# Setup in fixed order, grad_out requested by ScalarE, V0 in one load and head 31 stored in halves, in an attention backward kernel

## The chip, the cores and the metric

The kernel runs on one core of a Trainium2 chip. The metric is the device time of one execution in microseconds (us). Most executions agree within 0.3%, and every comparison is with runs of the kernel before on the same chip.

## The reference

Decode attention for 32 heads, one query row each, 8192 keys, width 128, all bfloat16, and its gradients:

```python
B, H, Sq, Skv, Dh = 1, 32, 1, 8192, 128
def _fwd_reference(q, k, v):
    scale = q.shape[-1] ** -0.5
    scores = jnp.einsum('bhqd,bhkd->bhqk', q, k) * scale
    attn = _softmax(scores, axis=-1)
    return jnp.einsum('bhqk,bhkd->bhqd', attn, v)
# returns out_0 = forward result, then the gradients for q, k, v:
_out, _vjp = jax.vjp(_f, q, k, v); _grads = _vjp(grad_out)
```

Per head K and V (2 MB each) are read, and dk and dv (2 MB each) are written. out and dq are one row per head.

## The kernel before

Each head: VectorE transposes K in four pieces, TensorE makes the scores, a softmax follows, TensorE transposes V (ScalarE copies it out of PSUM) and forms V·grad_out, and VectorE writes dv and dk as outer products. All transfers are asked for by SyncE, in one queue. The parts that the change and the argument touch:

```python
    def load_v(h):
        Vt[h] = vpool.tile([P, NT, D], BF16, tag="V", name="Vt")
        parts = NCH if h == 0 else 1                       # NCH = 4
        for c in range(parts):
            nc.sync.dma_start(slots(Vt[h], c, parts), rows_of(v, h, c, parts))

    rows = consts.tile([H, 2, D], BF16)
    nc.sync.dma_start(rows[:, 0, :], q.rearrange("b h s d -> (b h s) d"))
    nc.sync.dma_start(rows[:, 1, :], grad_out.rearrange("b h s d -> (b h s) d"))
    load_k(0); load_v(0); load_k(1); load_v(1)
    # ... setup: ident_f, ones_f, in_quad, lane; q columns (q_blk); grad_out columns
    #     (do_blk, do_f), all copies on VectorE; the scheduler chooses their order ...
    order = tc.manual_schedule()                           # from here on: order as written
    order.__enter__()

    def contract(Xt, rep, out_col, first=0, last=NT):      # o and dq: 64 one-column matmuls each
        for n in range(first, last):
            nc.tensor.matmul(out_col, lhsT=Xt[:, n, :], rhs=rep[:, n, 0:1],
                             start=(n == 0), stop=(n == NT - 1), skip_group_check=True)

    def outer(h, which, r):                                # quarter r of dk or dv
        # ... VectorE multiply into G ...
        parts = 4 if h == H - 1 else 2 if h == 0 else 1
        if r % (4 // parts) == 4 // parts - 1:
            c = r // (4 // parts)
            nc.sync.dma_start(rows_of(dst, h, c, parts), slots(G, c, parts))
```

## Time and profile before

| | before |
|---|---|
| time, median (range) | 649.27 us (648.69 to 650.84) |
| span in the profile | 647.3 us |
| HBM traffic, mean rate | 269.81 MB, 417 GB/s |
| TensorE, VectorE, ScalarE busy | 78%, 79%, 28% |
| last landing of a transfer | 646.28 us |

How to read it: in the lines, PE, DVE, ACT, POOL and SP are TensorE, VectorE, ScalarE, GpSimd and SyncE, and a q behind the name is the part of the engine that issues requests. K0 is K of head 0, V31 is V of head 31. The rate in forty slices tells where time is lost; the table of stretches with DMA share tells by how many DMA engines it is lost. The trace records sixteen landings for each large transfer, one for each DMA engine. I call the difference between the last and the first of them the lag. No view prints them one by one, so these are given as numbers. The lines themselves stand in the prediction.

### The profile page before, as it was taken

What the parts mean: (1) busy time and instruction counts of PE and PEld (TensorE: products, weight loads), DVE (VectorE), ACT (ScalarE), POOL (GpSimd) and SP (SyncE); (2) the same over time, 40 slices, a digit from 0 to 9 for tenths busy, and PEclk for the clock granted to TensorE, in tenths of its full rate; (3) what the DMA queues carried; (4) which work ended last, traced back from release to release, by engine and by line L of the source; (5) the groups of instructions that cost most, each with busy time, mean ns of one, the idle gap of its engine ahead of it and who ended that gap; (6) DMA issues with size and microseconds to landing.
All of it is one profiled execution on the core that took longest, in us unless ns stands there. A gap on an engine that the chain in (4) does not pass through costs nothing.

```text
span 647.3 us, 20978 instructions
## 1 busy us (share of the span) xinstructions
PE 505.1 (78%) x9705; PEld 472.7 (73%) x9705; DVE 513.1 (79%) x660; ACT 183.1 (28%) x325; POOL 0.7 (0%) x6
## 2 busy tenths in 40 slices
PE   2888888788968787888768787768887777977970
PEld 1888788688867777878668787668886776877870
DVE  5799889789977779777788777797777977778860
ACT  0333223223333222232222332222322223222240
POOL 0000000000000000000000000000000000000000
PEclk9866555556676555656565565575556666555565
DMA  8999999999999999999999999999999999999984
GB/s 329 413 425 428 424 427 427 426 426 425 428 427 429 426 429 426 431 424 430 425 430 426 431 424 430 430 425 422 426 425 429 427 430 425 427 431 428 409 367 201
DMA packets 20727, 269.81 MB, mean 417 GB/s; under 512 B 2464, under 2 KB 2464, under 8 KB 4512
## 3 DMA queue, kind: packets, MB, share of 16 engines
q1 hardware_dynamic: 20640, 268.48, 97.9%
q8 instruction: 76, 1.25, 0.7%
q14 instruction: 11, 0.09, 0.0%
HBM read 134.23 MB, written 134.23 MB: 415 GB/s over the span
## 4 chain that ended last, share of the span: by engine, by line
DMA 53%; PE 29%; DVE 11%; ACT 3%; issue 1%; SPq 0%; DVEq 0%; ACTq 0%
DMA Kt<-in_k_dram 48%; PE T_ps L179 10%; DVE XK_sb L141 8%; PE s_ps L153 6%; PE dp_ps L196 5%; DMA out_dram<-G_dv 5%; PE m_ps L196 2%; PE dp_ps L191 2%; ACT XT_sb L181 1%; PE s_ps L169 1%; PE m_ps L273 1%; PE m_ps L286 1%; DVE G_dv L206 1%; ACT e L285 1%; ACT qd L222 1%
## 5 line engine op out<-in xcount | busy, mean ns | idle before, releaser
L179 PE MATMUL T_ps<-ident_f,Vt 128*128 128x128 f32 x1024 | 220.4, 396 | 0.0
L206 DVE TENSOR_TENSOR G_dv<-p_rep,qd 128x2048 bf16<-128x2048 bf16 x128 | 148.2, 1221 | 68.5 <-DMA out_dram<-G_dv 66.0
L179 PEld LDWEIGHTS T_ps<-ident_f,Vt 128*128 128x128 f32 x1024 | 195.1, 216 | 0.0
L181 ACT COPY XT_sb<-T_ps 128x1024 f32<-128x1024 f32 x128 | 129.6, 1013 | 145.8 <-PE T_ps L179 145.8
L206 DVE TENSOR_TENSOR G_dk<-ds_rep,qd 128x2048 bf16<-128x2048 bf16 x128 | 155.8, 1219 | 1.1
L141 DVE STREAM_TRANSPOSE XK_sb<-Kt 128x1024 f32<-128x1024 f32 x128 | 148.1, 1214 | 5.6 <-DMA Kt<-in_k_dram 5.5
L153 PE MATMUL s_ps<-q_blk,XK_sb 128*128 128x4 bf16 x2048 | 59.6, 168 | 45.8 <-DVE pdt L227 43.0
L191 PEld LDWEIGHTS <-XT_sb 128*128 128x128 bf16 x2048 | 72.2, 105 | 28.6 <-ACT XT_sb L181 27.0
L191 PE MATMUL dp_ps<-do_blk,XT_sb 128*128 128x2 bf16 x2048 | 73.0, 165 | 24.3 <-ACT XT_sb L181 24.3
L153 PEld LDWEIGHTS <-XK_sb 128*128 128x128 bf16 x2048 | 57.1, 104 | 47.7 <-DVE pdt L227 44.9
L196 PE MATMUL dp_ps<-ds_rep,Kt 128*128 128x1 bf16 x2048 | 64.6, 165 | 3.8 <-issue 3.4
L196 PEld LDWEIGHTS <-Kt 128*128 128x128 bf16 x2048 | 59.8, 104 | 9.5 <-issue 9.4
L196 PEld LDWEIGHTS <-Vt 128*128 128x128 bf16 x2048 | 60.2, 101 | 1.6
L237 ACT COPY dq_all<-dp_ps 128x1 f32<-128x1 f32 x32 | 5.1, 159 | 193.4 <-PE dp_ps L196 193.4
L196 PE MATMUL m_ps<-p_rep,Vt 128*128 128x1 bf16 x2048 | 58.7, 165 | 0.0
L286 PEld LDWEIGHTS m_ps<-rs,ones_f 128*128 128x128 f32 x64 | 16.0, 309 | 48.6 <-ACT e L285 48.6
L286 PE MATMUL m_ps<-rs,ones_f 128*128 128x1 f32 x64 | 18.7, 361 | 39.2 <-ACT e L285 39.2
L273 PE MATMUL m_ps<-diag,ones_f 128*128 128x128 f32 x64 | 25.5, 499 | 2.0 <-issue 1.3
L282 DVE TENSOR_REDUCE nbias<-m_ps 128x1 f32<-128x128 f32 x32 | 9.3, 292 | 21.6 <-ACT qd L222 21.6
L295 ACT ACTIVATE p_rep<-e,rinv 128x256 bf16<-128x256 f32 x32 | 16.3, 508 | 30.3 <-DVE rinv L293 30.3
L222 ACT CAST qd<-m_ps 128x256 bf16<-128x256 f32 x32 | 11.9, 372 | 44.8 <-PE m_ps L218 44.8
L229 DVE SCALAR_TENSOR_TENSOR ds_rep<-dp_ps,pdt,p_s 128x256 bf16<-128x256 f32 x32 | 15.5, 484 | 10.3 <-PE dp_ps L191 8.0
(44 smaller groups left out, 155.1 us busy)
## 6 DMA issues: line engine op xcount, KB each, us to landing
Kt<-in_k_dram SPq DMA_DIRECT2D x31, 2048.0 KB, 30.8
Vt<-in_v_dram SPq DMA_DIRECT2D x31, 2048.0 KB, 28.2
out_dram<-G_dv SPq DMA_DIRECT2D x30, 2048.0 KB, 32.7
out_dram<-G_dk SPq DMA_DIRECT2D x30, 2048.0 KB, 33.0
Kt<-in_k_dram SPq DMA_DIRECT2D x4, 512.0 KB, 5.2
Vt<-in_v_dram SPq DMA_DIRECT2D x4, 512.0 KB, 8.1
out_dram<-G_dv SPq DMA_DIRECT2D x2, 1024.0 KB, 11.0
out_dram<-G_dk SPq DMA_DIRECT2D x2, 1024.0 KB, 12.4
```

Of the source, the lines that this page charges most:

```text
L141: nc.vector.transpose(XK[h][:, :, :, u, :], slots(Kt[h], u, NCH).rearrange("p g d -> p (g d)").bitcast(F32).rearrange("p (g w j) -> p g w ...
L153: nc.tensor.matmul(out[:, g, :], lhsT=cols[:, g, c // 2, c % 2], rhs=q_blk[:, h, c, :], start=(c == 0), stop=(c == 2 * NB - 1), skip_group ...
L179: nc.tensor.transpose(T_ps[:, i, :], words[:, m * P:(m + 1) * P], ident_f[:])
L181: nc.scalar.copy(X[:], T_ps[:])
L191: nc.tensor.matmul(st[h]["dp"][:, n:n + 2], lhsT=X[:, i, e2, :], rhs=do_blk[:, h, e2, :], start=(e2 == 0), stop=(e2 == 1), skip_group_chec ...
L196: nc.tensor.matmul(out_col, lhsT=Xt[:, n, :], rhs=rep[:, n, 0:1], start=(n == 0), stop=(n == NT - 1), skip_group_check=True)
L206: nc.vector.tensor_tensor(slots(G, r, 4).rearrange("p n (a b) -> p n a b", b=R), slots(rep, r, 4).unsqueeze(2).to_broadcast([P, Q, D // R, ...
L222: nc.scalar.copy(x["qd"][:].rearrange("p a d -> p (a d)"), x["m"][:, 256:512])
L229: nc.vector.scalar_tensor_tensor(out=x["ds"][:], in0=x["dp"][:, 0:NT].unsqueeze(2).to_broadcast([P, NT, R]), scalar=pdt[:], in1=x["p_s"][: ...
L273: nc.tensor.matmul(x["m"][:, 128:256], lhsT=ones_f[:], rhs=diag[:], start=True, stop=True, skip_group_check=True)
L286: nc.tensor.matmul(x["m"][:, 0:1], lhsT=ones_f[:], rhs=rs[:], start=True, stop=True, skip_group_check=True)
L295: nc.scalar.activation(x["p"][:], e[:].unsqueeze(2).to_broadcast([P, NT, R]), ACT.Copy, scale=rinv[:])
```

## The change

The intent: make the q columns while K0 is in flight and not in the middle of its transposes; take grad_out's request out of the way of K0's; move grad_out's columns to ScalarE; have fewer, larger requests at both ends.

```diff
     def load_v(h):
         Vt[h] = vpool.tile([P, NT, D], BF16, tag="V", name="Vt")
-        parts = NCH if h == 0 else 1
-        for c in range(parts):
-            nc.sync.dma_start(slots(Vt[h], c, parts), rows_of(v, h, c, parts))
+        nc.sync.dma_start(Vt[h][:], rows_of(v, h, 0, 1))
@@
-    nc.sync.dma_start(rows[:, 1, :], grad_out.rearrange("b h s d -> (b h s) d"))
+    nc.scalar.dma_start(rows[:, 1, :], grad_out.rearrange("b h s d -> (b h s) d"))
@@ the fixed order now begins ahead of the setup
+    order = tc.manual_schedule()
+    order.__enter__()
@@ q columns: four copies, four transposes into one PSUM tile, four products; (cut)
@@ grad_out columns: from VectorE to ScalarE, after head 0's scores
+    def do_columns():
+        for e2 in range(2):
+            nc.scalar.copy(twice[:, e2], ...)
+        ... three transposes ...
+        for e2 in range(2):
+            for t in range(2):
+                nc.scalar.copy(do_blk[t * W:(t + 1) * W, :, e2, t], ...)
+        nc.scalar.copy(do_f[:], tp[:, 2, 0:H])
@@ in outer()
-        parts = 4 if h == H - 1 else 2 if h == 0 else 1
+        parts = 1
+        if h == 0 or h == H - 1:
+            parts = 2
@@ in the loop over heads
+        if h == 0:
+            do_columns()
```

More of the change, by code (lines that the diff above doesn't have):

```diff
@@ L91 @@
     make_identity(nc, ident[:])
+    order = tc.manual_schedule()
+    order.__enter__()
+    ones_f = consts.tile([P, P], F32)
+    nc.vector.memset(ones_f[:], 1.0)
+    do_blk = consts.tile([P, H, 2, 2], BF16)
+    nc.vector.memset(do_blk[:], 0.0)
+    in_quad = consts.tile([P, NQ], F32)
+    nc.vector.reduce_sum(in_quad[:], ident[:].rearrange("p (a i) -> p a i", a=NQ), axis=AX.X)
+    q_blk = consts.tile([P, H, 2 * NB, NQ], BF16)
+    four = consts.tile([H, 2 * NB, NQ, QD], BF16)
+    for w in range(NB):
+        for e2 in range(2):
+            nc.vector.tensor_copy(
+                four[:, 2 * w + e2], rows[:, 0, :].rearrange("h (w j e) -> h w e j", w=NB, e=2)[:, w, e2:e2 + 1, :]
+                .to_broadcast([H, NQ, QD]))
@@ L92 @@
+    tp = psT.tile([P, CH, P], BF16, tag="T", name="tp_q")
+    for c in range(2 * NB):
+        nc.tensor.transpose(tp[:, c, 0:H], four[:, c].rearrange("h a j -> h (a j)"), ident[0:H, 0:H])
+    lane = consts.tile([P, QD], F32)
+    nc.vector.reduce_sum(lane[:], ident[:].rearrange("p (a i) -> p i a", a=NQ), axis=AX.X)
     ident_f = consts.tile([P, P], F32)
     nc.vector.tensor_copy(ident_f[:], ident[:])
-    ones_f = consts.tile([P, P], F32)
-    nc.vector.memset(ones_f[:], 1.0)
-    in_quad = consts.tile([P, NQ], F32)
@@ L97 @@
-    nc.vector.reduce_sum(in_quad[:], ident[:].rearrange("p (a i) -> p a i", a=NQ), axis=AX.X)
-    lane = consts.tile([P, QD], F32)
-    nc.vector.reduce_sum(lane[:], ident[:].rearrange("p (a i) -> p i a", a=NQ), axis=AX.X)
-    q_blk = consts.tile([P, H, 2 * NB, NQ], BF16)
-    for w in range(NB):
-        for e2 in range(2):
-            four = consts.tile([H, NQ, QD], BF16, tag=f"four{w}{e2}")
-            nc.vector.tensor_copy(
-                four[:], rows[:, 0, :].rearrange("h (w j e) -> h w e j", w=NB, e=2)[:, w, e2:e2 + 1, :]
-                .to_broadcast([H, NQ, QD]))
-            tp = psT.tile([P, CH, P], BF16, tag="T")
-            nc.tensor.transpose(tp[:, 0, 0:H], four[:].rearrange("h a j -> h (a j)"), ident[0:H, 0:H])
-            nc.vector.tensor_tensor(
-                q_blk[:, :, 2 * w + e2, :], tp[:, 0, 0:H].unsqueeze(2).to_broadcast([P, H, NQ]),
-                in_quad[:].unsqueeze(1).to_broadcast([P, H, NQ]), op=ALU.mult)
@@ L115 @@
-    do_blk = consts.tile([P, H, 2, 2], BF16)
-    nc.vector.memset(do_blk[:], 0.0)
-    for e2 in range(2):
-        twice = consts.tile([H, 2, W], BF16, tag=f"twice{e2}")
-        nc.vector.tensor_copy(
-            twice[:], rows[:, 1, :].rearrange("h (j e) -> h e j", e=2)[:, e2:e2 + 1, :].to_broadcast([H, 2, W]))
-        tp = psT.tile([P, CH, P], BF16, tag="T")
-        nc.tensor.transpose(tp[:, 0, 0:H], twice[:].rearrange("h t j -> h (t j)"), ident[0:H, 0:H])
-        for t in range(2):
-            nc.vector.tensor_copy(do_blk[t * W:(t + 1) * W, :, e2, t], tp[t * W:(t + 1) * W, 0, 0:H])
@@ L125 @@
-    do_f = consts.tile([P, H], F32)
-    tp = psT.tile([P, CH, P], BF16, tag="T")
-    nc.tensor.transpose(tp[:, 0, 0:H], rows[:, 1, :], ident[0:H, 0:H])
-    nc.vector.tensor_copy(do_f[:], tp[:, 0, 0:H])
+    for c in range(2 * NB):
+        nc.vector.tensor_tensor(
+            q_blk[:, :, c, :], tp[:, c, 0:H].unsqueeze(2).to_broadcast([P, H, NQ]),
+            in_quad[:].unsqueeze(1).to_broadcast([P, H, NQ]), op=ALU.mult)
+    twice = consts.tile([H, 2, 2, W], BF16)
+    do_f = consts.tile([P, H], F32)
@@ new lines, in do_columns @@
+    def do_columns():
+        for e2 in range(2):
+            nc.scalar.copy(
+                twice[:, e2], rows[:, 1, :].rearrange("h (j e) -> h e j", e=2)[:, e2:e2 + 1, :].to_broadcast([H, 2, W]))
+        tp = psT.tile([P, CH, P], BF16, tag="T", name="tp_do")
+        for e2 in range(2):
+            nc.tensor.transpose(tp[:, e2, 0:H], twice[:, e2].rearrange("h t j -> h (t j)"), ident[0:H, 0:H])
+        nc.tensor.transpose(tp[:, 2, 0:H], rows[:, 1, :], ident[0:H, 0:H])
+        for e2 in range(2):
+            for t in range(2):
+                nc.scalar.copy(do_blk[t * W:(t + 1) * W, :, e2, t], tp[t * W:(t + 1) * W, e2, 0:H])
+        nc.scalar.copy(do_f[:], tp[:, 2, 0:H])
@@ L130 @@
     o_all = consts.tile([P, H], F32)
     dq_all = consts.tile([P, H], F32)
-    order = tc.manual_schedule()
-    order.__enter__()
     def k_blocks(h, u):
```

## The prediction

> **What bounds the kernel now.** I read the page of the profile first. It moves 269.81 MB at a mean of 417 GB/s, while no compute engine is busy for more than 79% of the span.
>
> ```profile
> span 647.3 us, 20978 instructions
> PE 505.1 (78%) x9705; PEld 472.7 (73%) x9705; DVE 513.1 (79%) x660; ACT 183.1 (28%) x325; POOL 0.7 (0%) x6
> DMA  8999999999999999999999999999999999999984
> GB/s 329 413 425 428 424 427 427 426 426 425 428 427 429 426 429 426 431 424 430 425 430 426 431 424 430 430 425 422 426 425 429 427 430 425 427 431 428 409 367 201
> DMA 53%; PE 29%; DVE 11%; ACT 3%; issue 1%; SPq 0%; DVEq 0%; ACTq 0%
> ```
>
> The reader is to see a flat row of GB/s, about 427, between a poor first slice (329) and three poor last ones (409, 367, 201). At 427 GB/s the traffic needs 269.81 / 0.427 = 632 us of the 647.3, so all that the change can touch is some 15 us at the two ends. The DMA share of the chain of waits says the same of the middle.
>
> Next the timeline of the start, which is where most of the diff works:
>
> ```profile
> 1.19 0.41 SPq L84 DMA_DIRECT2D rows<-in_grad_out_dram  x1
> 1.65 1.85 SPq L74 DMA_DIRECT2D Kt<-in_k_dram  x4
> ...
> 5.53 2.52 DVE L141 STREAM_TRANSPOSE XK_sb<-Kt 128x1024 f32<-128x1024 f32 x2 [2.16 <-DMA Kt<-in_k_dram]
> ...
> 8.54 1.04 DVE L111 TENSOR_TENSOR q_blk<-tp,in_quad 128x128 bf16<-128x128 bf16 x4
> ...
> 10.76 2.36 DVE L141 STREAM_TRANSPOSE XK_sb<-Kt 128x1024 f32<-128x1024 f32 x2
> ```
>
> VectorE transposes half of K0, then makes the q and grad_out columns from 7.97 to 10.84, then the other half of K0: the setup sits in the middle of head 0. And grad_out's request delays K0's first request from 1.19 to 1.65 us.
>
> Then the timeline of the end, and the table of stretches over it:
>
> ```profile
> 620.47 4.63 DVE L206 TENSOR_TENSOR G_dv<-p_rep,qd 128x2048 bf16<-128x2048 bf16 x4 [2.98 <-DMA out_dram<-G_dv]
> ...
> 629.03 8.77 SPq L214 DMA_DIRECT2D out_dram<-G_dk  x4
> ...
> 638.69 0.33 SPq L246 DMA_DIRECT2D out_dram<-fin_sb  x1
> ```
>
> ```profile
> 638.00:640.00 2.00, 0.00 (x0) 0.00 (x0) 0.00 (x0) 0.00 (x0) 0.00 (x0) 0.50 0.95 381
> 640.00:642.00 2.00, 0.00 (x0) 0.00 (x0) 0.00 (x0) 0.00 (x0) 0.00 (x0) 0.50 0.42 172
> 642.00:644.00 2.00, 0.00 (x0) 0.00 (x0) 0.00 (x0) 0.00 (x0) 0.00 (x0) 0.50 0.13 52
> 644.00:646.00 2.00, 0.00 (x0) 0.00 (x0) 0.00 (x0) 0.00 (x0) 0.00 (x0) 0.50 0.05 21
> ```
>
> These four rows (last two columns: DMA share, GB/s) decide my prediction. Compute ended at about 632.4, the last large request went out at 637.5, and yet data moves until 645.7 with a share that sinks to 0.05. One engine of sixteen is 0.06, and one sixteenth of 427 GB/s is 27. So at the end a single DMA engine is still working off a backlog and the other fifteen are done. I checked it in the landing records of the trace, of which each transfer has sixteen. The first and the last of the sixteen are 0.6 us apart for K0, 2.1 for K2, 8.2 at 200 us, 17.0 for V31. And the last one never pauses: K31, the dk of head 29, V31, the dv of 30, the dk of 30 in two transfers are finished at 605.3, 610.5, 615.4, 620.4, 625.8, 631.3, 636.1 in the order of the queue, always about 5 us for 2 MB; then 512 KB quarters follow each other every 1.23 to 1.26 us up to 646.1. In the middle it is the same, 4.87 us for a load and 5.0 to 5.1 for a store. The dips at 612 to 620 and 628 to 640 us are those of the engines that ran ahead and had nothing left; the late one was never without work from 5 us on.
>
> So what bounds the kernel is the slowest DMA engine: its first byte, plus its sixteenth of everything (with whatever else it carries), plus a last microsecond of closing.
>
> **What the Trainium skill says.** "DMA: Bandwidth & Descriptors", section "Why a DMA increments its semaphore by 16 and not by 1": a transfer runs on up to 16 engines that finish independently, and only the full count means that all has landed. The trace agrees: sixteen landings per transfer, up to 17 us apart. The same page, section "Issuing engines are not separate DMA queues": requests from ScalarE and SyncE run on the same 16 engines, and a second issuer saves only sequencer time. For grad_out that time is visible here, 0.46 us between two SyncE requests (1.19 to 1.65). "Runtime: NRT & Kernel Launch", section "Instruction fetch mechanics": an engine's instructions arrive by DMA in 16 KiB blocks. The page's DMA table agrees (queue 8, kind instruction: 76 packets, 1.25 MB); they ride on the same engines and are my guess at why some of those lag. The change hardly alters the number of instructions, so it leaves them alone.
>
> **The change, part by part.**
>
> (a) grad_out requested by ScalarE. K0's first request moves from 1.65 to 1.19, and everything behind it in the one queue with it: **-0.46 us** on the path of the slow engine. ScalarE's request stands ahead of its table load (0.73, 1.28 us), which nobody waits for.
>
> (b) The setup in fixed order. VectorE has before K0: in_quad 0.28, four copies 0.62, lane 0.36, ident_f 0.18, four q products 1.04 = 2.5 us. q landed at 2.46, so the copies end near 3.1, TensorE's four small transposes near 3.6, the products near 4.9. K0's first chunk then lands at 5.51 - 0.46 = 5.05: it fits, barely. The chunks land at 5.05, 6.3, 7.8 and 9.05; four transposes of 1.22 end near 10.3 instead of 13.12, so head 0's scores start 2.9 us earlier. The grad_out columns go to ScalarE: seven small copies, which I estimate at 0.2 to 0.3 us each from its 128x32 cast of 0.22 and 128x256 cast of 0.37, together about 1.7 us; two come while it waits for K0, five after the scores, and ScalarE is idle until 15 us anyway. That head start is real for compute and worth **0 us** at the end: the requests in the one queue keep their order (K0, V0, K1, V1, K2, dv0, V2, dk0, ...), the first five are 10 MB or about 25 us of DMA work, to roughly 28.5 us, and the first half of dv0 was already requested at 22.83. It will be at about 20 and lie longer in the queue.
>
> (c) V0 in one load. The slow engine took 1.28 + 1.27 + 1.28 + 1.26 = 5.09 us for V0 in four parts of 512 KB, and 4.87 for a load of 2 MB: **-0.2 us**. V0 is complete near 14 us and first needed by TensorE near 16.4 (19.25 - 2.9), so that waiting for all of it costs nothing.
>
> (d) Head 31 in halves. Before, ten requests lie at the end (four dv, out_0, four dk, out_1), and each waits for the eighth before it. That is why the four dk requests stretch over 8.77 us and out_1's comes at 638.69. In the list of SyncE's waits this is
>
> ```profile
> SPq L214 <- DMA out_dram<-G_dk: 4.5, 1, 4.5
> SPq L214 <- DMA out_dram<-G_dv: 2.8, 2, 1.9
> ```
>
> With six requests the eighth before landed long ago; the last half of dk31 is requested at 632.5 as soon as VectorE has made it, 5 us earlier, and out_1 right after. Does the slow engine feel it? No: at 632.5 it is still at dk30 (lands 636.1) and has dv31 before it. It gains only the form of the packets: the quarters took 5.01 us for dv31 and 4.75 for dk31 (642.41 - 641.36, then 1.24, 1.22, 1.23), and halves of head 0 took 2.79 + 2.12 and 2.33 + 2.44, about 4.85 for 2 MB. I book **-0.1 us**. The other engines finish earlier, which ends nothing.
>
> Sum: -0.46 - 0 - 0.2 - 0.1 = -0.76 us; 649.27 - 0.76 = **648.5 us**.
>
> **The rivals.** First, the head start counts: if the queue of some engine ran dry between 20 and 32 us, 2.9 us of earlier stores and loads would be worth part of that. For it speaks the rate from 26 to 28 us, 344 GB/s; against it the landings there, which go on at 4.9 to 5.6 us per 2 MB on the late engine with three requests waiting. It would give about 646. Second, the end is set by the late requests: if the wait of the last dk quarters (5 us) were on the path, the time would fall to some 644. For it speaks the chain of waits, which passes through head 31; against it the share of 0.05 at the end and landings every 1.23 us without a gap. Third, a loss: halves start later than quarters (the first dv half 1.2 us later, the first dk half 1.2 us later), or V0 in one piece delays the first transposes. The slow engine has 10 us of backlog at that point, so neither shows; it would need the backlog to be gone, and would cost 1 to 2 us. Fourth, VectorE's q products slip behind K0's first chunk, by up to 1 us; this is hidden by the same queue.
>
> **Range and chances.** The three runs of before span 648.69 to 650.84, so noise is about as large as the gain. Weighing 0.7 for my sum, 0.2 for the first two rivals and 0.1 for a loss or a slow draw, 8 in 10 lie within 646.3 to 650.0. Two per cent is 13 us: nearly all that the two ends hold. Faster by over 2%: 0.02; within: 0.97; slower: 0.01.
>
> **What would show it.** K0's first request near 1.19 and its first transpose near 5.05; all four transposes in a row, ending near 10.3; the last dk request near 632.5 with no wait of SyncE on an earlier store; and still a tail of sinking share to about 645, the last transfers landing 10 us and more after their requests. If the rows of the last 8 us fill up instead, or the end follows the last request by 5 us, the second rival was right; if the end moves by over 2 us with an unchanged tail, the first. I would be wrong at the root if the late engine turned out to have pauses, or if its lag depends on what the requests look like.

## The result, and the profile after

The changed kernel took 648.18 us (median of 4 runs, 648.10 to 648.41); the kernel before 649.37 (median of 4, 648.69 to 650.84). The ratio is 0.9979, 95% interval 0.9962 to 0.9997. Here and below a ratio is the mean time of one kernel's runs over that of the other's of the same rounds, so it isn't quite the ratio of the medians. Five later runs of the changed kernel gave 0.9979 again (0.9966 to 0.9991). So it is faster by about 1.4 us or 0.2%, within the 2% that count as the same.

The page of the changed kernel, its span and the DMA rows:

```profile
span 646.4 us, 20967 instructions
DMA  8999999999999999999999999999999999999985
GB/s 341 415 426 427 427 420 425 431 424 426 427 428 428 427 431 424 427 430 428 427 428 431 425 427 429 429 429 426 427 429 426 428 429 428 425 429 430 409 358 216
```

Its instruction fetches, which matter further down (packets, MB, share of the 16 engines' time):

```profile
q8 instruction: 76, 1.25, 0.7%
q14 instruction: 11, 0.09, 0.0%
```

The plateau is the same, the first slice went from 329 to 341, and the last three are as poor as they were (409, 358, 216). Its timeline at the start (start, duration, engine, line, operation):

```profile
0.73 0.42 ACTq L82 DMA_DIRECT2D rows<-in_grad_out_dram  x1
...
1.19 1.83 SPq L74 DMA_DIRECT2D Kt<-in_k_dram  x4
...
4.85 1.25 DVE L146 STREAM_TRANSPOSE XK_sb<-Kt 128x1024 f32<-128x1024 f32 x1 [0.71 <-DMA Kt<-in_k_dram]
6.30 1.25 DVE L146 STREAM_TRANSPOSE XK_sb<-Kt 128x1024 f32<-128x1024 f32 x1 [0.21 <-DMA Kt<-in_k_dram]
8.50 2.46 DVE L146 STREAM_TRANSPOSE XK_sb<-Kt 128x1024 f32<-128x1024 f32 x2 [0.94 <-DMA Kt<-in_k_dram]
```

K0 is requested at 1.19 and VectorE waits for nothing but K0: the setup is out of the way. Head 0's scores start at 11.01 us in place of 13.17 (at 10.35 in a second trace of the changed kernel). And the end, first the timeline, then the table of stretches (last two columns DMA share and GB/s):

```profile
630.81 2.60 SPq L221 DMA_DIRECT2D out_dram<-G_dk  x2
...
633.51 0.48 SPq L253 DMA_DIRECT2D out_dram<-fin_sb  x1
```

```profile
640.00:642.00 2.00, 0.00 (x0) 0.00 (x0) 0.00 (x0) 0.00 (x0) 0.00 (x0) 0.50 0.28 117
642.00:644.00 2.00, 0.00 (x0) 0.00 (x0) 0.00 (x0) 0.00 (x0) 0.00 (x0) 0.50 0.06 25
644.00:646.00 2.00, 0.00 (x0) 0.00 (x0) 0.00 (x0) 0.00 (x0) 0.00 (x0) 0.50 0.02 8
```

All requests are out by 634 (before: 639), yet data moves for eleven more microseconds, in the last of them with a share of one engine in sixteen (0.06) or less. The last landing came at 645.35, 0.93 us before that of the kernel before.

### The profile page after: what moved, and what is told of

Its sections match the earlier page's. It is cut to its first block, busy times and chain, and to the rows that moved or that the text cites. A ratio compares the mean times of both kernels' runs of the same rounds, so it can differ in the third digit from the quotient of the medians.

```text
span 646.4 us, 20967 instructions
## 1 busy us (share of the span) xinstructions
PE 500.6 (77%) x9705; PEld 468.8 (73%) x9705; DVE 512.2 (79%) x653; ACT 184.7 (29%) x332; POOL 0.7 (0%) x6
## 3 DMA queue, kind: packets, MB, share of 16 engines
q8 instruction: 76, 1.25, 0.7%
## 4 chain that ended last, share of the span: by engine, by line
DMA 58%; PE 23%; DVE 13%; ACT 2%; issue 1%; SPq 0%; DVEq 0%; ACTq 0%
DMA Kt<-in_k_dram 58%; DVE XK_sb L146 10%; PE T_ps L184 6%; PE s_ps L158 6%; PE dp_ps L201 5%; PE m_ps L201 2%; DVE G_dv L211 1%; PE dp_ps L196 1%; PE s_ps L174 1%; ACT XT_sb L186 1%; PE m_ps L282 1%; DVE G_dk L211 1%; PE m_ps L295 1%; ACT qd L229 0%; PE m_ps L225 0%
## 5 line engine op out<-in xcount | busy, mean ns | idle before, releaser
L184 PE MATMUL T_ps<-ident_f,Vt 128*128 128x128 f32 x1024 | 216.2, 391 | 0.0
L184 PEld LDWEIGHTS T_ps<-ident_f,Vt 128*128 128x128 f32 x1024 | 191.8, 213 | 0.0
```

The lines of the kernel that those rows point to most:

```text
L184: nc.tensor.transpose(T_ps[:, i, :], words[:, m * P:(m + 1) * P], ident_f[:])
```

## The experiments

Two questions. Which part of the change moved the end, and is the single late DMA engine really what sets it; and if so, what makes it late? The landings, read from each run's trace:

| trace | last landing, us | lag at V31, us |
|---|---|---|
| before; before again | 646.28; 646.91 | 17.0; 16.2 |
| changed; changed again | 645.35; 644.59 | 16.6; 15.9 |
| setup order only | 645.66 | 16.6 |
| grad_out by ScalarE and V0 in one load only | 645.58 | 15.6 |
| halves only | 646.15 | 17.3 |
| out_0 in five pieces | 645.19 | 16.9 |
| fewer TensorE instructions | 638.48 | 9.6 |
| more GpSimd instructions | 652.11 | 21.0 |
| shift; control; cut along the row | 656.91; 667.33; 653.66 | 6.0; 28.5; 3.7 |

Two traces of one kernel differ by 0.6 to 0.8 us, so a single landing tells nothing below that.

**The kernel before, a second trace** (one look, 649.76 us, beside 649.49 of the kernel before in its own run).

> The kernel before once more, for a second trace of it: last landing within 0.6 us of 646.3 (the traces of the kernels with the same requests so far ended at 645.6 to 646.3), K0's first landing 5.3 to 5.5 us.

The last landing was 646.91, just outside the 0.6 allowed. K0's first landing was 4.83; the 5.3 to 5.5 of the expectation fits only the completion of K0's first chunk, at 5.42. The 0.6 us between the two traces are the size of chance.

**The setup order alone.** From the changed kernel, the other parts undone:

```diff
-    nc.scalar.dma_start(rows[:, 1, :], ...)
+    nc.sync.dma_start(rows[:, 1, :], ...)
@@ load_v: V0 in NCH parts again;  outer: head 31 in quarters again
```

> The kernel before with only the setup in fixed order and the grad_out columns on ScalarE (grad_out still asked for by SyncE, V0 still in four loads, head 31 still in quarters). My theory (the slowest DMA engine, never without work, sets the end): head 0's scores start 2 to 3 us earlier, the last landing stays within 0.4 us of the 646.3 of the kernel before, ratio 0.999 to 1.001. The rival that the head start counts: the end moves by 1.5 to 3 us, ratio 0.995 to 0.998.

Measured: 648.93 us (5 runs) against 649.26, ratio 0.9990 (0.9977 to 1.0003). VectorE's timeline in this run:

```profile
5.34 2.54 DVE L148 STREAM_TRANSPOSE XK_sb<-Kt 128x1024 f32<-128x1024 f32 x2 [1.09 <-DMA Kt<-in_k_dram]
8.31 2.50 DVE L148 STREAM_TRANSPOSE XK_sb<-Kt 128x1024 f32<-128x1024 f32 x2 [0.42 <-DMA Kt<-in_k_dram]
```

The last of K0's transposes ends at 10.81, not 13.12: a head start of 2.3 us, as meant. The last landing moved by 0.62 to 1.25 us (against the two traces of before), more than the 0.4 that I had allowed, though less than the rival's 1.5 to 3; the interval of the times includes no gain at all. A gain of some tenths is not excluded.

**grad_out by ScalarE and V0 in one load, alone.** From the kernel before:

```diff
-    nc.sync.dma_start(rows[:, 1, :], ...)
+    nc.scalar.dma_start(rows[:, 1, :], ...)
@@ load_v
-        parts = NCH if h == 0 else 1
-        for c in range(parts): ...
+        nc.sync.dma_start(Vt[h][:], rows_of(v, h, 0, 1))
```

> The kernel before with only grad_out asked for by ScalarE and V0 in one load. My theory: first landing of K0 0.4 to 0.7 us earlier, and the end 0.5 to 0.9 us earlier (last landing about 645.6), ratio 0.9985 to 0.9993; the compute of head 0 moves by no more than that. Rival (the gain of the change came from the setup order): last landing unchanged, ratio 1.000.

Measured: 649.29 us (5 runs) against 649.26, ratio 0.9994 (0.9982 to 1.0007). K0's first landing came at 4.42 in place of 4.87 and 4.83, V0 took the last engine 4.90 us in place of 5.09, and the last landing came at 645.58. The landings are as expected; the ratio is just outside the expected range, and the times can't tell it from nothing.

**Head 31 in halves, alone.** From the kernel before, only the lines of outer() from the change.

> The kernel before with only head 31's stores in halves. My theory: the last dk request goes out about 5 us earlier (632 to 633 in place of 637.5), the last landing moves by 0.0 to 0.3 us only, ratio 0.9995 to 1.000; the landings of the slowest engine follow one another to the end without a gap. Rival (the late requests are on the path): the end moves by 2 to 5 us, ratio 0.992 to 0.997.

Measured: 648.88 us (5 runs) against 649.26, ratio 0.9993 (0.9979 to 1.0007). SyncE's timeline and the table of stretches:

```profile
629.16 2.60 SPq L216 DMA_DIRECT2D out_dram<-G_dk  x2
631.86 0.41 SPq L248 DMA_DIRECT2D out_dram<-fin_sb  x1
```

```profile
642.00:644.00 2.00, 0.00 (x0) 0.00 (x0) 0.00 (x0) 0.00 (x0) 0.00 (x0) 0.50 0.09 37
644.00:646.00 2.00, 0.00 (x0) 0.00 (x0) 0.00 (x0) 0.00 (x0) 0.00 (x0) 0.50 0.04 17
```

The last dk request went out at 631.43, six us earlier than before, and the last landing at 646.15 is where it was. The six us were waited by SyncE; nobody else felt them.

**out_0 in five pieces.** From the changed kernel; the opposite test of the same rival, and a probe of which engines are late. Only out_0 is stored in pieces, not out_1.

```diff
-        nc.sync.dma_start(dst..., fin_sb[:])                 # 32 rows
+        for n in (1, 3, 7, 8, 13):
+            nc.sync.dma_start(dst...[at:at + n, :], fin_sb[at:at + n, :]); at += n
```

> The changed kernel with the 8 KB store of out_0 in five requests of 1, 3, 7, 8 and 13 rows. Two questions. (1) With four requests more at the end, the two dk requests of head 31 wait for an earlier store and go out at about 635.5 and 638 in place of 630.8 and 633.1. My theory: the slowest engine reaches them only after that, so the time stays within 0.5 us of the changed kernel's 648.2. The rival that late requests cost: 2 to 4 us longer. (2) [...]the landings of the five pieces, which stand in each engine's queue behind its share of the large stores, tell which engines are late: if engines 0 to 6 are the early ones, the pieces of 1, 3 and 7 rows land near 629 to 631; if they are the late ones, near 638 to 641.

Measured: 647.78 us (4 runs), ratio 0.9980 (0.9965 to 0.9995), as the changed kernel. The requests of dk did come late:

```profile
628.17 2.33 SPq L255 DMA_DIRECT2D out_dram<-fin_sb  x5
635.21 2.80 SPq L221 DMA_DIRECT2D out_dram<-G_dk  x2
640.12 0.33 SPq L255 DMA_DIRECT2D out_dram<-fin_sb  x1
```

Over four us later than in the changed kernel, and no time lost. That the late requests are on the path is refuted from both sides. The probe: the piece of 1 row landed at 629.2; that of 3 at 629.6; of the piece of 7, four landings came at 629.9 and three at 636.5, 636.7 and 640.3; the piece of 8 had one early landing more and the same three late ones; of the 13, six by 631.8, six from 635.1 to 637.1, one at 640.6. (Each piece has one more record, 0.4 to 0.5 us after its request and ahead of these; it is left out here.) By the Trainium skill ("DMA: Bandwidth & Descriptors", section "Why a DMA increments its semaphore by 16 and not by 1") such a request runs on the lowest-numbered n engines; the numbers of landings agree. If so, engines 0, 1, 2 and 7 are early, and the latest is one of 3 to 6.

**Fewer TensorE instructions.** From the changed kernel; the results are wrong, the transfers are the same.

```diff
     def contract(Xt, rep, out_col, first=0, last=NT):
-        for n in range(first, last):
+        for n in [m for m in range(first, last) if m in (0, NT // 2 - 1, NT // 2, NT - 1)]:
```

> The changed kernel with 124 of the 128 one-column matmuls per head of the o and dq contractions left out (wrong out_0, out_1, dk on purpose; same transfers). TensorE has 7,700 instructions fewer, so about 30 instruction packets of 16 KB fewer of 76. If instruction fetch makes the slow engine slow: its lag behind the first one at V31 falls from 16.6 us to 8 to 11, and the end comes 4 to 8 us earlier, ratio to before 0.986 to 0.992. Rival (the lag is of the engines themselves or of the stores): lag 15 to 18 us, ratio 0.997 to 0.999, though TensorE is busy for some 100 us less.

Measured: 641.35 us (4 runs) against 649.26, ratio 0.9878 (0.9865 to 0.9892). The page of this run:

```profile
span 639.5 us, 13287 instructions
PE 375.2 (59%) x5865; PEld 339.9 (53%) x5865; DVE 512.7 (80%) x653; ACT 181.6 (28%) x332; POOL 0.7 (0%) x6
GB/s 346 411 422 428 429 422 420 427 426 429 425 433 428 427 430 429 431 424 434 428 427 430 431 426 429 429 428 430 427 429 430 427 431 427 428 434 426 427 427 243
q8 instruction: 46, 0.75, 0.4%
```

30 instruction packets fewer, lag 9.6 in place of 16.6, and the second and third last slices are full (427 in place of 409 and 358). The plateau in the middle has not risen: the gain is that the engines finish closer together. But TensorE also works 125 us less, so this run alone doesn't say whether it was the fetch or the work.

**More GpSimd instructions** separates the two: TensorE as in the changed kernel, and one-element memsets on the idle GpSimd.

```diff
+    spare = consts.tile([1, 1], F32)
+    for _ in range(9728):            # second attempt: 4200
+        nc.gpsimd.memset(spare[:], 0.0)
```

> The changed kernel with 9,728 one-element memsets on GpSimd, which nothing waits for: 0.62 MB more of instructions, about 38 packets of 16 KB more (114 in place of 76). If instruction fetch slows engines and GpSimd's fetches go to the same ones as TensorE's: lag at V31 25 us in place of 16.6 and the end 6 to 9 us later, ratio to before 1.007 to 1.012. If they go to other engines: the spread changes its shape, the end moves by less than 3 us. If fetch is innocent: nothing moves.

The first attempt measured 1433.05 us (ratio 2.2076) and says nothing of the time: GpSimd started a memset every 0.15 us, not every 0.03 as I had read off the first four. Its trace was of use up to head 31, for the next expectation.

> As the run with 9,728 memsets, which GpSimd itself drew out to 1,431 us, but with 4,200 of them, so that GpSimd ends near 620 us: about 33 instruction packets of 8 KB more. In the long run two engines came to lag by 20.0 and 22.0 us at V31 in place of 14.7 and 16.6, and the data of head 31 landed at 652.8 in place of 645.4. Fetch theory: the same here, last landing 651.5 to 653, ratio to before 1.007 to 1.011. If fetch is innocent: ratio 0.997 to 0.999.

Measured: 655.58 us (4 runs) against 649.31, ratio 1.0099 (1.0086 to 1.0112). Two lines of the DMA table and the last stretches:

```profile
q8 instruction: 76, 1.25, 0.8%
q14 instruction: 44, 0.36, 0.1%
```

```profile
640.00:644.00 4.00, 0.00 (x0) 0.00 (x0) 0.00 (x0) 0.00 (x0) 0.00 (x0) 0.50 0.76 311
644.00:648.00 4.00, 0.00 (x0) 0.00 (x0) 0.00 (x0) 0.00 (x0) 0.00 (x0) 0.50 0.13 53
648.00:652.00 4.00, 0.00 (x0) 0.00 (x0) 0.00 (x0) 0.00 (x0) 0.00 (x0) 0.50 0.06 25
```

33 packets of 8 KB more (44 in place of 11), and a core that moves the same data and does the same arithmetic takes over 7 us longer than the changed kernel (647.85 us in the same rounds), at the end on one engine (share 0.06). Two engines have moved out to a lag of 19.1 and 21.0; the third last stands at 12.0. With the run before it, the end moved in both directions with the number of fetches: about 6.1 us earlier for 30 packets of 16 KB fewer (638.48 against 644.59), 7.5 us later for 33 packets of 8 KB more, which by the shape of the lag fell on two engines (652.11 against 644.59).

Each of the two runs changes something besides the fetches: the first also TensorE's work, the second also what GpSimd writes. The starts of the packets settle which it was. In the ten traces of the table above its last line, queue 8 begins its first fetch at 19.7 to 23.2 us. From V0 to K1, both landed by then, the lag grows in none of them: in the kernel before it is 0.59 us at V0 and 0.55 at K1. V1, in flight when the first fetch comes, has a lag of 1.68, but fifteen of its landings lie within 0.56 us: one engine alone was delayed. In all ten traces the lag grows from K1 to V1, by 0.5 to 1.7 us. With more GpSimd instructions, memsets run from 0.9 us on, yet V0 alone, in flight when queue 14 begins its first packet at 11.4 us, shows a jump: from 0.55 at K0's last chunk to 0.87, again on one engine (the other fifteen lie within 0.56). In the two traces of the changed kernel, where that packet comes at 49 us, the lag is the same at both.

The sizes agree too. Added over the sixteen engines, the delay behind the first at V31 is 137.7 us after 72 fetches of queue 8 in the kernel before, 132.4 after 73 in the changed one and 79.7 after 44 with fewer TensorE instructions: 1.8 to 1.9 us a fetch in each. It fell by 40% with the fetches, while TensorE's busy time fell by 25%.

**An attempt to use it.** If engines 0 to 2 are early, a request of 3 rows gives them work and takes it from the rest. From the changed kernel, in outer(), for the dk of heads 8, 13, 18, 23 and 28:

```diff
+            cuts = [112] + [3] * 5 + [1]      # shift;  control: [96, 16, 16]
+            for n in cuts:
+                nc.sync.dma_start(rows_of(...)[at:at + n], slots(...)[at:at + n]); at += n
```

with the changed kernel in the same rounds as the measure (647.85 us, ratio 0.9979):

> The changed kernel once more, unaltered, for the size of chance and as the measure for the next two: ratio 0.9975 to 0.999, last landing within 0.4 us of 645.4, lag of the last engine at V31 16 to 17.5 us.

The ratio is as expected; the last landing, 644.59, was 0.8 us early and the lag, 15.9, just under its range. Chance between two traces is thus larger than I had allowed.

> The changed kernel with work shifted from the late engines to three early ones: in five heads (8, 13, 18, 23, 28) the dk store goes out as 112 rows on all sixteen engines (7 each) and 16 rows in requests of 3, 3, 3, 3, 3 and 1[...]. Thirteen engines carry 5 rows of 16 KB less, at 0.61 us a row (4.9 us for 8 rows): my theory says the end comes 2.4 to 3.1 us before that of the changed kernel, last landing 642.2 to 643.0, ratio to before 0.993 to 0.9955. If the engines' balance is not what sets the end, or the waits of the thirty more requests cost: ratio 0.998 or over.

> The control of the shift: the same five dk stores in three requests of 96, 16 and 16 rows, each on all sixteen engines, so no engine carries less. Theory: no gain over the changed kernel, within 0.4 us of it, ratio to before 0.9975 to 0.9995. If splitting alone helped, it would follow the shift to 0.993 to 0.9955.

Both failed: the shift took 660.11 us (ratio 1.0178, 1.0160 to 1.0197), the control 668.13 (1.0279, 1.0239 to 1.0319). So cutting a store by partitions cost far more here than the 2.4 to 3.1 us that the balance was to give, and the two runs can't tell whether shifting as such works. In the control the dv store of head 8, which stands in the queue ahead of the first cut store, already took the late engine 7.57 us in place of 5.0 while the early engines were at the cut one. The third variant cuts the same stores into as many requests as the shift, but along the row, so that each has all 128 partitions (`[:, at:at + n, :]` with n = 10, 9, 9, 9, 9, 9, 9).

> Why the shift and its control were slower: the same five dk stores of the changed kernel in seven requests each, as many as in the shift, but cut along the row (10 and six times 9 of the 64 pieces of a row), so that each request has all 128 partitions. If requests of few partitions are what cost[...]: no loss, within 0.6 us of the changed kernel, ratio to before 0.997 to 0.9995. If the number of requests and their waits for the eighth before them cost: ratio 1.01 to 1.03, as in those two.

Measured: 656.42 us (5 runs) against 648.81, ratio 1.0108 (1.0094 to 1.0122): at the low end of the range that I had set for the number of requests. That cannot be all, since the shift with as many requests lost 1.8% and the control with only three lost 2.8%. SyncE's timeline shows what the number of requests does:

```profile
177.15 25.25 SPq L226 DMA_DIRECT2D out_dram<-G_dk  x7
207.04 0.34 SPq L78 DMA_DIRECT2D Vt<-in_v_dram  x1
```

Each request waits for the eighth before it (the program uses eight completion semaphores in turn, as the semaphore numbers in the trace show; this is the program's way, not a limit of the chip that was measured), so the seven take until 202 and the V load goes out at 207.04 where otherwise it would have been out near 190 (a head takes 20 us, and the V load before it went out at 170). The early engines run dry (the lag falls from 8.2 to 3.4 us), and in each of the five heads the V load reaches the last engine 6.0 to 6.6 us after the transfer before it, not 4.87: 1.1 to 1.8 us lost, 7.3 in all, of the 9.1 by which this trace ends later than that of the changed kernel (653.66 against 644.59). What the cuts by partitions (shift and control) cost beyond that is left, by elimination, to requests of fewer than 128 partitions; that rows 96 to 111 and 112 to 127 reach only 4 of the 16 SBUF ports each (the Trainium skill, "SBUF — State Buffer", section "Door 1: The DMA port swizzle") fits the control's 7.57 us, but no run isolates it. No version that beats the changed kernel came out of this: the one with fewer instructions is wrong in its results.

## Why the prediction was right

**What bounds the kernel.** Right: a last stretch with a share of about one engine ends every variant whose stretches are shown, and the end went with the late engine: 638.5 with 30 fetches fewer, 652.1 with 33 more, unmoved by requests 6 us earlier or 4 us later. The guess that instruction fetch is what makes engines late is now shown by two runs in opposite directions and by the jumps of the lag at the first fetches. Two readings were loose. The seven transfers that end at 605.3 to 636.1 are K31, the dk of head 28, V31, the dv and dk of head 29 and the dv and dk of head 30, 4.9 to 5.5 us apart. And the backlog when the first dv half of head 0 is requested (22.83) reaches to 31.11, 8 us and not 10. Neither enters the sum.

**(a) grad_out by ScalarE**, booked at 0.46 us: K0's first landing came at 4.83 to 4.87 in the four traces with grad_out on SyncE and at 4.19 to 4.43 in the ten with it on ScalarE, 0.4 to 0.7 us earlier. Right for the first landing. That the last engine gains as much is not shown: with (c), V0 should be complete 0.66 us earlier; it was at 14.59 and 13.93 in the two traces of the changed kernel, against 14.60 and 14.57 before.

**(b) Setup order**, booked at 0 for the end: the head start was 2.2 us in the first trace, where the third chunk of K0 landed late, at 8.47, and 2.8 in the second, where the chunks came nearly as predicted. Alone it gave 0.9990 with 1 inside the interval. The runs don't settle it: none, or some tenths of a microsecond.

**(c) V0 in one load**, booked at 0.2: 5.09 became 4.90. Right.

**(d) Halves**, booked at 0.1: dv31 took 4.92 in place of 5.01, dk31 4.71 in place of 4.75. Right, and the six us by which the request moved were indeed worth nothing.

**The sum**, 0.76 us, lies inside both measured intervals, 0.2 to 2.5 and 0.6 to 2.2 us, though their middle is 1.4. The three parts alone gave 0.9990, 0.9994 and 0.9993, which add up to the 0.9977 or so of the whole, but the interval of each includes no gain. So the parts are right by landings, not by times. The remaining 0.6 is as large as the difference between two traces of one kernel; whether (b) has a share in it stays open. That so small a sum fell inside the range says little, since any account of a gain of some tenths would have; the account of the late engine rests on the runs that moved the end by 6 to 8 us.

The rivals: the end set by late requests is refuted by the halves and by the pieces; the loss did not come; the head start is at most a fraction of what the rival gave it. The q products didn't slip: they ended at 4.13, and K0's first chunk was complete at 4.83.

**Where its reasoning would have misled:** it took for granted that a late request costs nothing while the last engine has work. At the end that held: in the run with out_0 in pieces the two dk stores were requested 5 us before the last engine came to them. In the middle, in the run with stores cut along the row, V was requested 5 us before the last engine had finished the pieces, and 1.1 to 1.8 us were lost all the same. That one is a load and the other a store is a difference; whether it is the cause was not tried. The prediction had also named a sign of being wrong at the root: a lag that depends on what the requests look like. Between the shapes that the change uses it doesn't (15.6 to 17.3 us at V31), but with cut stores in the middle it does: 3.7, 6.0 and 28.5 us. The account holds for this change and not for any shape of request.

## What to carry to other kernels

In a kernel that the DMA bounds, look at the DMA share of the last microseconds before you plan anything. A share of one engine in sixteen says that the end is a backlog of one engine. Here requests 6 us earlier then gained nothing, and a head start of the compute at most some tenths; what moved the end was what else rode on that engine. Instructions did: 30 fetches of TensorE fewer (with less work) ended the kernel 6 us earlier and 33 of GpSimd more ended it 7 us later, though neither engine bounds it. So count an unrolled kernel's instructions. And count requests before cutting a transfer: here each waits for the eighth before it. Cutting stores by partitions lost 1.8% and 2.8% here; measure before you do it.

## What the Trainium skill lacked or had wrong

- "Runtime: NRT & Kernel Launch", section "Instruction fetch mechanics", calls the cost of a fetch mostly hidden. It doesn't say what a fetch costs the transfers on the same DMA engines. In this kernel that wasn't hidden: 76 packets of TensorE's instructions, about 1.8 us of delay each when added over the engines, and the last engine 16 to 17 us behind the first at V31; 30 fewer (with less work on TensorE) ended the kernel 6.1 us earlier, 33 more on GpSimd 7.5 us later.
- The same section gives blocks of 16 KiB, 256 instructions. For TensorE the runs agree (2 x 9705 / 256 = 75.8, seen 76; 2 x 5865 / 256 = 45.8, seen 46). GpSimd's came in packets of 8,192 bytes: 4,200 memsets gave 33 more, 128 to a packet.
- "DMA: Bandwidth & Descriptors", section "Latency and other measured facts", says that engines 7 and 15 are usually slower; its guess at the cause applies only to transfers that GpSimd asks for, and here SyncE and ScalarE ask for all. Engine 7 was among the early ones and the latest was one of 3 to 6, as far as the requests of 1, 3, 7, 8 and 13 rows tell.
- No page says what the wait of a request for the eighth before it does: nothing at the end of this kernel (0.9980 with late requests, 0.9979 without); where it delayed a load in the middle, 1.1 to 1.8 us were lost in each such head. The wait itself is the program's, which has eight completion semaphores.
